# Second batch, chunks 0, 2 and 4: scores times v in three bfloat16 pieces instead of float32

## The chip, the cores and the metric

One Trainium2 chip, and one of its cores. The metric is the device time of one execution in microseconds (us): the median of several runs. The engines are PE (matrix products), PEld (PE's weight loads), DVE (vector), ACT (scalar), POOL (GpSimd) and SP, which issues all transfers (DMA) here. Each engine works through its own queue in order and waits on semaphores for the others.

## The reference

An attention with gates, 4 batches of 8 heads, 768 steps and 40 channels, and behind it a mixer of tokens and channels, all in float32:

```python
for t in range(S):
    m_new = np.maximum(f_gate[:, :, t] + m, i_gate[:, :, t])
    C = f_stab * C + i_stab * np.einsum('bhd,bhe->bhde', vt, kt)
    n = f_stab * n + i_stab * kt
    h_tilde = np.einsum('bhde,bhe->bhd', C, qt)
    denom = np.maximum(np.abs(nq), 1.0)          # nq: n times qt
    y[:, :, t] = o * h_tilde / denom             # o: sigmoid of o_gate
h = np.maximum(xt @ w_tok1, 0.0) @ w_tok2        # xt: y with steps last
u = x + h.transpose(0, 2, 1)
h2 = np.maximum(u @ w_ch1, 0.0) @ w_ch2
return (u + h2)
```

## The kernel before

A unit `(b, c)` is a batch `b` and a chunk `c` of 128 steps; there are 4 times 6. For a unit, PE makes the scores of 8 heads (`st_s`, tile `ps_sc`, L268). DVE multiplies them by decay weights (`st_p`, L278, two halves of four heads, in place in tile `dd`), which ACT has made as exponentials (`prep_exp`, L248, by halves) from what POOL has masked (`prep_mask`, L240). PE then multiplies the result by v with a column of ones (`st_pv`): 8 float32 products of 41 columns (L376), each two records in the trace. The share of the earlier chunks comes from a state `C` (product with q at L328 or L362; the update `pu` is L336 on PE, L340 and L344 on DVE). DVE divides (`st_norm`, L393 to L397, tile `x`), POOL multiplies by the gate (L404), ACT and POOL split x in two parts (`xh` L413, `xl` L418).

In the third and fourth batch (`three(u)`) the product with v is made in another way. The decayed scores are cut into three bfloat16 pieces: the upper 16 bits of the number as it stands, the upper 16 bits of the rest `r` (`prep_p2`, L290, two halves), and the rest of that (`prep_p3`, L298, two halves). v is cut into three as well (`prep_v`, L306 to L309, all on DVE). PE makes four bfloat16 products for a head (`st_pv3`, L357) into two PSUM tiles, ACT copies one column group (L364) and DVE adds the other (L365).

The mixer's products are L577, in dense streams: `gemm1` (tile `ps_h`, 16 products of 256 columns, read by ACT at L644 and by DVE at L645, tile `gl`) and `gemm2` (tile `acc`, two halves of 6 products of 320 columns; when a sum over 6 is ready, DVE adds it at L660 and so frees its PSUM bank). The order around the change is written out by hand. The attention of a batch is a generator, `att(b)`, with five pieces for a chunk: (0) scores, multiplication, `prep_p2`; (1) `prep_p3`, state; (2) exponentials of the next chunk's first half, its q and its weighted k; (3) product with v, `st_norm`; (4) `prep_v` of the next chunk, exponentials of its second half, loads. Batch 1 runs through its 30 pieces during the last six of the 18 steps of batch 0's mixer (`STEPS0`: how many pieces stand behind `gemm1`, behind the first and behind the second half of `gemm2`). Chunk 0's piece 0 stands one step earlier. PSUM pool `ps_m` has two banks, for `pu`, `po` and, in that one step, for two sums of `gemm2`.

Of the kernel before, what the change touches and what calls it, by code (L numbers as in the profile page):

```python
# [19 lines left out]
NC = S // L  # L20
# [14 lines left out]
def kernel(ctx: ExitStack, tc: tile.TileContext, gates, qk, q3, kv, og,  # L35
# [16 lines left out]
    def load_sig(b, i):  # L52
        t = ap.tile([128, NC // 2, DM], F32, tag="sig", name="sig", bufs=3)
        nc.sync.dma_start(out=t, in_=og[b].rearrange("(c p) e -> p c e", p=128)[:, 3 * i:3 * i + 3, :])
        sig[(b, i)] = t
# [93 lines left out]
    def top(x, i=1):  # L149
        return x.bitcast(BF16).rearrange("... (t i) -> ... t i", i=2)[..., i]  # L150
# [29 lines left out]
    def sigmoid(b, r=range(2), part=slice(0, 3)):  # L180
        for i in r:
            t = sig[(b, i)][:, part]
            nc.scalar.activation(t, t, AF.Sigmoid)
# [3 lines left out]
    def load_qk(u, hf):  # L187
        b, c = u
        t = T.setdefault(u, {})
        if hf == 0:  # L190
            t["raw"] = ap.tile([128, 2, 4, L], F32, tag="raw", name="raw", bufs=3)
        nc.sync.dma_start(out=t["raw"][64 * hf:64 * hf + D], in_=qk[b, c, hf])

    def load_phi(u):
        b, c = u
        T.setdefault(u, {})
        dd = ap.tile([128, H, L], F32, tag="dd", name="dd", bufs=3)
        if b:
            nc.sync.dma_start(out=dd, in_=phi_d[c, b * HP:b * HP + H].partition_broadcast(128))
        T[u]["dd"] = dd  # L200
# [7 lines left out]
    def load_q3(u):  # L208
        b, c = u
        if c > 0:  # L210
            load_pq(u, load_q3t(u))
# [16 lines left out]
    def prep_q3(u):  # L228
        if u[1] == 0:
            return  # L230
        q3t, pq = T[u]["q3"]
        nc.scalar.activation(pq, T[u].get("psq", pq), AF.Exp)  # L232
        if u[1] < NC - 1:
            T[u]["decay"] = a = ap.tile([120, 3], F32, tag="decay", name="decay")
            nc.gpsimd.tensor_copy(a, pq[:, :, L - 1])  # L235
        nc.gpsimd.tensor_tensor(q3t, q3t, pq, ALU.mult)  # L236

    def prep_mask(u):
        dd = T[u]["dd"]
        nc.gpsimd.affine_select(dd, dd, pattern=[[0, H], [1, L]], compare_op=ALU.is_ge,  # L240
                                fill=-1e30, base=0, channel_multiplier=-1)

    def prep_exp(u, hf):
        b, c = u
        dd = T[u]["dd"]
        src = T[u].get("phi")
        for h in range(4 * hf, 4 * hf + 4):
            nc.scalar.activation(dd[:, h, :], src[hf][:, h % 4, :] if src else dd[:, h, :], AF.Exp,  # L248
                                 bias=bcol[:, c, HP * b + h:HP * b + h + 1])

    def prep_kw(u):
        b, c = u
        if c == NC - 1:
            return
        t = T[u]
        kw = ap.tile([128, H * E1], F32, tag="kw", name="kw", bufs=2)
        kw = kw[:, 0:DM].rearrange("p (h d) -> p h d", d=D)
        nc.gpsimd.tensor_tensor(kw, t["kv"][:, 0:DM].rearrange("p (h d) -> p h d", d=D),
                                wcol[:, c, HP * b:HP * b + H].unsqueeze(2).to_broadcast([128, H, D]), ALU.mult)
        t["kw"] = kw  # L260

    def st_s(u, mult=True, mid=iter(())):
        t = T[u]
        t["s"] = [ps_s.tile([128, 4, L], F32, tag="s", name="ps_sc") for _ in range(2)]
        for h in range(4):
            for hf in range(2):
                r = t["raw"][64 * hf:64 * hf + D]
                nc.tensor.matmul(t["s"][hf][:, h, :], r[:, 1, h, :], r[:, 0, h, :], start=True, stop=True)  # L268
        if mult:
            st_p(u, mid)  # L270
# [7 lines left out]
            nc.vector.tensor_tensor(dd, t["s"][hf], dd, ALU.mult)  # L278

    def three(u):  # L280
        return u[0] > 1

    def prep_p2(u):
        t = T[u]
        dd = t["dd"]
        r = xpool[1].tile([128, H, L], F32, tag="p12", name="r", bufs=1)
        t["p"] = (top(dd), top(r), top(dd, 0))
        for hf in range(2):
            h = slice(4 * hf, 4 * hf + 4)
            nc.vector.tensor_tensor(r[:, h], dd[:, h], top(dd)[:, h], ALU.subtract)  # L290
        t["r"] = r

    def prep_p3(u):
        t = T[u]
        r, p3 = t["r"], t["p"][2]
        for hf in range(2):
            h = slice(4 * hf, 4 * hf + 4)
            nc.vector.tensor_tensor(p3[:, h], r[:, h], top(r)[:, h], ALU.subtract)  # L298

    def prep_v(u):  # L300
        t = T[u]
        vx = t["kv"][:, DM:]
        w = xpool[1].tile([128, 3, H * E1], BF16, tag="v3", name="v3", bufs=1)
        r = ap.tile([128, H * E1], F32, tag="kw", name="vr", bufs=2)
        v = nc.vector
        v.tensor_copy(w[:, 0], vx)  # L306
        v.tensor_tensor(r, vx, w[:, 0], ALU.subtract)
        v.tensor_copy(w[:, 1], r)
        v.tensor_tensor(w[:, 2], r, w[:, 1], ALU.subtract)  # L309
        t["v"] = w  # L310
# [8 lines left out]
    def st_state(u):  # L319
        b, c = u  # L320
        t = T[u]
        vx = t["kv"][:, DM:]
        t["C"] = Cst.get(b)
        if c > 0 and not three(u):
            po = po_tile(u)
            pof = po.rearrange("p h e -> p (h e)")
            for g, (h0, n) in enumerate(GR):
                nc.tensor.matmul(pof[:, h0 * E1:(h0 + n) * E1], t["q3"][0][0:n * D, g, :],  # L328
                                 Cst[b][0:n * D, g * G3:g * G3 + n * E1], start=g == 0, stop=False)
            t["po"] = po  # L330
        if c < NC - 1:
            pu = ps_m.tile([120, 3, G3], F32, tag="m", name="pu")
            puf = pu.rearrange("p g e -> p (g e)")
            kwf = t["kw"].rearrange("p h d -> p (h d)")
            for g, (h0, n) in enumerate(GR):
                nc.tensor.matmul(pu[0:n * D, g, 0:n * E1], kwf[:, h0 * D:(h0 + n) * D],  # L336
                                 vx[:, h0 * E1:(h0 + n) * E1], start=True, stop=True)
            cn = ap.tile([120, 3 * G3], F32, tag="C", name="Cn")
            for (p, a, z) in ((120, 0, 2 * G3), (80, 2 * G3, 2 * G3 + 2 * E1)):
                nc.vector.tensor_tensor(cn[0:p, a:z], puf[0:p, a:z], bm_t[0:p, a:z], ALU.mult)  # L340
            if c > 0:
                for g, (h0, n) in enumerate(GR):
                    sl = (slice(0, n * D), slice(g * G3, g * G3 + n * E1))
                    nc.vector.scalar_tensor_tensor(cn[sl], Cst[b][sl], t["decay"][0:n * D, g:g + 1], cn[sl],  # L344
                                                   op0=ALU.mult, op1=ALU.add)
            Cst[b] = cn
# [74 lines left out]
    def st_x(u):  # L421
        st_xm(u)
        st_xh(u)
        st_xl(u)

    units = [(b, c) for b in range(B) for c in range(NC)]
    u0, u1 = units[0], units[1]

    def after(u, n):
        i = units.index(u) + n  # L430
        return units[i] if i < len(units) else None

    def att(b):
        for c in range(NC):
            u = (b, c)
            n1, n2 = after(u, 1), after(u, 2)
            th = three(u)
            if b + 1 < B and c in (3, 4):
                load_sig(b + 1, c - 3)
            if b > 1 and c == 0:  # L440
                sigmoid(b)
            st_s(u)
            if n2:
                load_phi(n2)
            if n1 and not three(u):
                prep_mask(n1)
            if n2:
                load_qk(n2, 0)
            if th:
                prep_p2(u)  # L450
            yield
            if th:
                prep_p3(u)
            st_state(u)
            if n1 and three(u):
                prep_mask(n1)
            yield
            if n1:
                prep_exp(n1, 0)
                prep_q3(n1)  # L460
                prep_kw(n1)
            if n2:
                load_qk(n2, 1)
            yield
            st_pv(u)
            st_norm(u)
            if not th:
                st_x(u)
            yield
            if n1 and three(n1):  # L470
                prep_v(n1)
            if th:
                st_x(u)
            if n1:
                prep_exp(n1, 1)
            if n2:
                load_kv(n2)
                load_q3(n2)
            yield
# [296 lines left out]
    for c in range(2, NC - 1):  # L776
        u, n1, n2 = (units[c + i] for i in range(3))
# [225 lines left out]
```

## Time and profile before

| | |
|---|---|
| median of 3 runs | 459.84 us (455.59 to 465.8) |
| the profiled execution, its span | 459.81 us, 458.0 us |
| busy share of the span | PE 96%, PEld 92%, DVE 66%, ACT 43%, POOL 28% |
| granted PE clock, 40 equal slices, tenths | 9867779999999999999999999999999999999999 |
| chain that ended last, by engine | PE 74%, DVE 12%, DMA 6%, ACT 3%, POOL 3% |

And the stage in which the second batch's attention runs, by stretches (busy us of each engine, granted clock):

| us | PE | DVE | ACT | POOL | clock |
|---|---|---|---|---|---|
| 122 to 130 | 7.97 of 8 | 5.08 | 2.86 | 0.00 | 1.00 |
| 130 to 139 | 8.90 of 9 | 5.22 | 3.90 | 4.62 | 1.00 |
| 139 to 148 | 9.00 of 9 | 4.18 | 4.10 | 4.58 | 1.00 |
| 148 to 156 | 7.74 of 8 | 4.56 | 3.92 | 4.57 | 1.00 |
| 156 to 165 | 9.00 of 9 | 4.52 | 3.92 | 4.60 | 1.00 |
| 165 to 173 | 6.98 of 8 | 3.25 | 3.92 | 4.44 | 1.00 |

The span is the time from the first to the last instruction. Matrix products are pipelined and their ends are modelled, so PE's pace is read from the starts of its rows. In the clock's row a 9 is 90% or more of full speed.

### The profile page before, as it was taken

How to read it: one execution, taken by the hardware profiler on the slowest of the kernel's cores; microseconds unless marked ns; L12 is line 12 of the kernel's file. 1: busy time of each engine (PE TensorE's matmuls, PEld its weight loads, DVE VectorE, ACT ScalarE, POOL GpSimd, SP SyncE). 2: the span in 40 equal slices, each digit the busy share in tenths (PEclk: the TensorE clock that was granted, in tenths of full speed). 3: DMA queues.
4: the chain of work that ended last, by engine and by line, in shares of the span. 5: the costliest groups of instructions: out<-in, count | busy, mean ns of one | idle time of the engine just before them, and what ended most of it. 6: DMA issues, size and time to landing. Idle time of an engine off the chain costs nothing.

```text
span 458.0 us, 9425 instructions
## 1 busy us (share of the span) xinstructions
PE 441.7 (96%) x3713; PEld 421.6 (92%) x3713; DVE 303.7 (66%) x652; ACT 197.9 (43%) x478; POOL 130.2 (28%) x158
## 2 busy tenths in 40 slices
PE   8997897998999999999999999999999999999997
PEld 3887796998999989999999999999999999999996
DVE  5868789787455446879788667978888735233212
ACT  3665657997535355443242425532434212112111
POOL 5406423545334652142214402332412210000000
PEclk9867779999999999999999999999999999999999
DMA  7845757865066864323344422413421000000000
GB/s 181 249 130 159 221 163 243 285 177 159 0 208 191 248 220 124 106 105 94 107 148 135 154 87 75 136 33 92 161 73 38 1 2 29 1 1 29 1 31 29
DMA packets 24910, 52.98 MB, mean 116 GB/s; under 512 B 2574, under 2 KB 13658, under 8 KB 24866
## 3 DMA queue, kind: packets, MB, share of 16 engines
q1 hardware_dynamic: 24818, 52.27, 37.2%
q8 instruction: 29, 0.48, 0.4%
q14 instruction: 15, 0.12, 0.1%
q10 hardware_dynamic: 48, 0.11, 0.1%
HBM read 48.33 MB, written 4.04 MB: 114 GB/s over the span
## 4 chain that ended last, share of the span: by engine, by line
PE 74%; DVE 12%; DMA 6%; ACT 3%; POOL 3%; issue 2%; SPq 1%; DVEq 0%; ACTq 0%; POOLq 0%
PE ps_h L577 24%; PE acc L577 23%; PE ps_a L577 5%; PE ps_sc L268 4%; PE ps_b L577 4%; PE po L376 4%; DMA pq<-phi_d 3%; DVE wf L550 3%; PE po L357 3%; PE pu L336 2%; PE po L362 2%; DVE wf L554 2%; DMA wst<-in_wc_dram 2%; DVE r L290 1%; POOL q3t L236 1%
## 5 line engine op out<-in xcount | busy, mean ns | idle before, releaser
L577 PE MATMUL ps_h<-uT,c1h 128*128 128x256 f32 x720 | 140.2, 282 | 1.6 <-DVE uT L628 1.6
L577 PEld LDWEIGHTS ps_h<-uT,c1h 128*128 128x128 f32 x720 | 115.4, 188 | 2.4 <-DVE uT L628 1.8
L577 PE MATMUL ps_h<-uT,c1l 128*128 128x256 f32 x432 | 111.4, 280 | 0.0
L644 ACT ACTIVATE gh<-ps_h 128x512 fp32r<-128x512 f32 x72 | 42.5, 591 | 138.9 <-PE ps_h L577 138.9
L645 DVE SCALAR_TENSOR_TENSOR gl<-ps_h,gh 128x512 fp32r<-128x512 f32 x72 | 49.6, 688 | 77.7 <-ACT gh L644 77.5
L577 PE MATMUL acc<-c2h,gh 128*128 128x320 f32 x288 | 90.5, 322 | 0.0
L577 PE MATMUL acc<-c2l,gh 128*128 128x320 f32 x288 | 86.7, 309 | 0.0
L577 PEld LDWEIGHTS ps_h<-uT,c1l 128*128 128x128 f32 x432 | 81.4, 188 | 0.0
L577 PE MATMUL acc<-c2h,gl 128*128 128x320 f32 x288 | 66.1, 310 | 1.4 <-DVE gl L645 1.4
L577 PEld LDWEIGHTS acc<-c2h,gh 128*128 128x128 f32 x288 | 54.1, 188 | 1.3
L577 PEld LDWEIGHTS acc<-c2l,gh 128*128 128x128 f32 x288 | 54.2, 188 | 0.0
L577 PEld LDWEIGHTS acc<-c2h,gl 128*128 128x128 f32 x288 | 47.9, 188 | 2.5 <-DVE gl L645 2.3
L248 ACT ACTIVATE dd<-dd,bcol 128x128 f32<-128x128 f32 x144 | 45.7, 389 | 1.5 <-POOL dd L240 1.5
L278 DVE TENSOR_TENSOR dd<-ps_sc,dd 128x512 f32<-128x512 f32 x48 | 31.2, 683 | 21.5 <-ACT dd L248 13.0
L404 POOL TENSOR_TENSOR x<-x,sig 128x320 f32<-128x320 f32 x23 | 20.8, 904 | 56.7 <-DVE x L397 56.7
L235 POOL COPY decay<-pq 120x3 f32<-120x3 f32 x16 | 3.3, 208 | 113.4 <-ACT pq L232 89.9
L413 ACT ACTIVATE xh<-x 128x320 fp32r<-128x320 f32 x24 | 11.3, 470 | 52.3 <-POOL x L404 50.4
L268 PE MATMUL ps_sc<-raw 40*128 40x128 f32 x384 | 31.2, 298 | 2.6 <-DMA raw<-in_qk_dram 2.5
L268 PEld LDWEIGHTS ps_sc<-raw 40*128 40x128 f32 x384 | 25.9, 198 | 6.8 <-issue 2.5
L376 PE MATMUL po<-kvt,dd 128*128 128x41 f32 x192 | 29.4, 307 | 1.3 <-DVE dd L278 1.3
L376 PEld LDWEIGHTS po<-kvt,dd 128*128 128x128 f32 x192 | 28.2, 222 | 2.5 <-DVE dd L278 1.5
L236 POOL TENSOR_TENSOR q3t<-q3t,pq 120x384 f32<-120x384 f32 x20 | 22.0, 1098 | 26.5 <-ACT pq L232 22.4
(123 smaller groups left out, 777.5 us busy)
## 6 DMA issues: line engine op xcount, KB each, us to landing
dd<-phi_d SPq DMA_DIRECT2D x18, 512.0 KB
wst<-in_wc_dram SPq DMA_DIRECT2D x22, 384.0 KB
kvt<-in_kv_dram SPq DMA_DIRECT2D x24, 324.0 KB
raw<-in_qk_dram SPq DMA_DIRECT2D x48, 160.0 KB
sig<-in_og_dram SPq DMA_DIRECT2D x8, 480.0 KB
out_dram<-x SPq DMA_DIRECT2D x24, 160.0 KB
q3t<-in_q_dram SPq DMA_DIRECT2D x20, 180.0 KB
wst<-in_wt_dram SPq DMA_DIRECT2D x8, 384.0 KB
```

What stands on the lines that cost most here:

```text
L236: nc.gpsimd.tensor_tensor(q3t, q3t, pq, ALU.mult)
L248: nc.scalar.activation(dd[:, h, :], src[hf][:, h % 4, :] if src else dd[:, h, :], AF.Exp, bias=bcol[:, c, HP * b + h:HP * b + h + 1])
L268: nc.tensor.matmul(t["s"][hf][:, h, :], r[:, 1, h, :], r[:, 0, h, :], start=True, stop=True)
L278: nc.vector.tensor_tensor(dd, t["s"][hf], dd, ALU.mult)
L357: nc.tensor.matmul(po[:, h - h0, 0:j1 - j0], p[i][:, ROW[h], :], w[:, h, j0:j1], start=h == h0 and i + j0 == 0, stop=c == 0 and h == h1 - ...
L376: nc.tensor.matmul(po[:, h, :], t["dd"][:, ROW[h], :], vx[:, h * E1:(h + 1) * E1], start=c == 0 and h == 0, stop=h == H - 1)
L404: eng.tensor_tensor(x, x, sig[(b, c // 3)][:, c % 3, :], ALU.mult)
L413: nc.scalar.activation(xh, x, AF.Copy)
L550: v.scalar_tensor_tensor(fi, fi, 3, raw[:, :, 0], op0=ALU.logical_shift_left, op1=ALU.bitwise_or)
L577: nc.tensor.matmul(ps, a, m, start=(first and i == 0), stop=(last and i == n - 1))
L644: nc.scalar.activation(gh, ps, AF.Relu)
L645: nc.vector.scalar_tensor_tensor(gl, ps, 0.0, f32(gh), op0=ALU.max, op1=ALU.subtract)
```

## The change

Units (1, 0), (1, 2) and (1, 4) go the way of the last two batches: scores and v in three bfloat16 pieces. Unit (1, 0) has no chunk before it in which `prep_v` could stand, so its `prep_v` stands behind its `prep_p2`. All follows from `three`, by which `att`, `st_state` and `st_pv` choose.

```diff
     def three(u):
-        return u[0] > 1
+        return u[0] > 1 or u[0] == 1 and u[1] % 2 == 0
@@ att(b), piece 0
             if th:
                 prep_p2(u)
+            if th and u == units[NC]:
+                prep_v(u)
             yield
             if th:
                 prep_p3(u)
```

The two added lines move the numbers of the lines below them by two (L645 becomes L647, L660 becomes L662). ACT's, POOL's and SP's orders stay as they were, but for six L364 on ACT.

DVE's queue around chunk 0 of the second batch; `acc` are two finished sums of the mixer, `gl` the remainder that the mixer's next product needs, `Cn` the state. Before:

```order
L278 TENSOR_TENSOR dd<-ps_sc,dd 128x512 x2
L645 SCALAR_TENSOR_TENSOR gl<-ps_h_1596,gh 128x512
L660 TENSOR_TENSOR x<-acc_1107,x 128x320
L660 TENSOR_TENSOR x<-acc_1108,x 128x320
L340 TENSOR_TENSOR Cn<-pu,bm_t 120x246
```

And with the change:

```order
L278 TENSOR_TENSOR dd<-ps_sc,dd 128x512 x2
L290 TENSOR_TENSOR r<-dd 128x512 x2
L306 CAST v_1596<-kvt 128x328
L307 TENSOR_TENSOR vr<-kvt,v_1596 128x328
L308 CAST v_1596<-vr 128x328
L309 TENSOR_TENSOR v_1596<-vr,v_1596 128x328
L647 SCALAR_TENSOR_TENSOR gl<-ps_h_1602,gh 128x512
L662 TENSOR_TENSOR x<-acc_1107,x 128x320
L662 TENSOR_TENSOR x<-acc_1108,x 128x320
L298 TENSOR_TENSOR dd<-r 128x512 x2
L340 TENSOR_TENSOR Cn<-pu,bm_t 120x246
```

Six operations now stand between the multiplication and the two additions that free PSUM banks, and two more between these and the state.

DVE's queue from chunk 1's division to chunk 2's state. Before:

```order
L397 TENSOR_TENSOR x<-po,den 128x320
L278 TENSOR_TENSOR dd<-ps_sc,dd 128x512 x2
L645 SCALAR_TENSOR_TENSOR gl<-ps_h_1808,gh 128x512
L340 TENSOR_TENSOR Cn<-pu,bm_t 120x246
L340 TENSOR_TENSOR Cn<-pu,bm_t 80x82
```

And with the change:

```order
L397 TENSOR_TENSOR x<-po,den 128x320
L306 CAST v_1814<-kvt 128x328
L307 TENSOR_TENSOR vr<-kvt,v_1814 128x328
L308 CAST v_1814<-vr 128x328
L309 TENSOR_TENSOR v_1814<-vr,v_1814 128x328
L278 TENSOR_TENSOR dd<-ps_sc,dd 128x512 x2
L290 TENSOR_TENSOR r<-dd 128x512 x2
L647 SCALAR_TENSOR_TENSOR gl<-ps_h_1855,gh 128x512
L298 TENSOR_TENSOR dd<-r 128x512 x2
L340 TENSOR_TENSOR Cn<-pu,bm_t 120x246
```

The split of v stands in front of the multiplication, L290 right behind it, and `gl` of the mixer between L290 and L298. Chunks 3 and 4 read the same.

## Rows read from the trace of the kernel before

**Rows 1.** Chain that ended last: start us, us, what.

```profile
137.33 1.73 PE po L376 x16
...
192.40 1.02 PE po L357 x32
```

**Rows 2.** PE's timeline: start, length (us), line, operation, out<-in, count [idle before].

```profile
132.81 1.16 PE L268 MATMUL ps_sc<-raw 40*128 40x128 f32 x16
...
138.87 0.39 PE L577 MATMUL acc<-c2h,gh 128*128 128x320 f32 x1
...
147.86 0.39 PE L577 MATMUL acc<-c2h,gh 128*128 128x320 f32 x1
...
155.43 0.39 PE L577 MATMUL acc<-c2h,gh 128*128 128x320 f32 x1
...
164.32 0.39 PE L577 MATMUL acc<-c2h,gh 128*128 128x320 f32 x1
...
170.68 1.53 PE L376 MATMUL po<-kvt,dd 128*128 128x41 f32 x12 [1.02 <-DVE dd L278]
...
172.04 0.39 PE L577 MATMUL acc<-c2h,gh 128*128 128x320 f32 x1
```

**Rows 3.** DVE's timeline, chunks 0 and 1 of the second batch.

```profile
126.22 1.29 DVE L278 TENSOR_TENSOR dd<-ps_sc,dd 128x512 f32<-128x512 f32 x2 [0.16 <-PE ps_sc L268]
...
129.74 1.01 DVE L660 TENSOR_TENSOR x<-acc,x 128x320 f32<-128x320 f32 x2
...
133.62 0.49 DVE L397 TENSOR_TENSOR x<-po,den 128x320 f32<-128x320 f32 x1
...
136.76 0.69 DVE L278 TENSOR_TENSOR dd<-ps_sc,dd 128x512 f32<-128x512 f32 x1 [1.97 <-ACT dd L248]
...
139.85 0.49 DVE L397 TENSOR_TENSOR x<-po,den 128x320 f32<-128x320 f32 x1
```

**Rows 4.** The split of v: DVE's timeline, and the view of line L307.

```profile
173.29 0.32 DVE L306 CAST v<-kvt 128x328 bf16<-128x328 f32 x1
...
175.10 1.06 DVE L309 TENSOR_TENSOR v<-vr,v 128x328 bf16<-128x328 f32 x1
...
L307 DVE TENSOR_TENSOR vr<-kvt,v x12: 501/984/1267, 173.7 to 360.6; 128x328 f32<-128x328 f32 x12
```

**Rows 5.** POOL's and DVE's timeline in the third batch.

```profile
203.62 1.02 POOL L236 TENSOR_TENSOR q3t<-q3t,pq 120x384 f32<-120x384 f32 x1
...
203.67 2.65 DVE L290 TENSOR_TENSOR r<-dd 128x512 f32<-128x512 f32 x2
...
206.24 1.36 DVE L298 TENSOR_TENSOR dd<-r 128x512 bf16<-128x512 f32 x2
...
217.44 1.28 DVE L290 TENSOR_TENSOR r<-dd 128x512 f32<-128x512 f32 x2
```

**Rows 6.** PE and DVE around the product in three pieces, third batch.

```profile
207.65 0.24 PE L357 MATMUL po<-v,dd 128*128 128x41 bf16 x2 [0.20 <-DVE dd L298]
...
209.07 0.39 PE L577 MATMUL acc<-c2h,gh 128*128 128x320 f32 x1
...
194.85 0.49 DVE L397 TENSOR_TENSOR x<-ht,den 128x320 f32<-128x320 f32 x1
```

**Rows 7.** PE's timeline where the clock fell or held; two stretches, PEclk third from last.

```profile
56.44 0.90 PE L328 MATMUL po<-Cn,q3t 120*128 120x123 f32 x6 [1.23 <-POOL q3t L236]
...
60.93 0.47 PE L577 MATMUL ps_a<-xh,w1l 128*128 128x320 f32 x1
...
64.40 0.37 PE L577 MATMUL ps_a<-xl,w1h 128*128 128x320 f32 x1
...
76.60 0.71 PE L577 MATMUL ps_h<-uT,c1h 128*128 128x256 f32 x3 [1.58 <-DVE uT L628]
...
58.00:59.00 1.00, 1.00 (x8) 1.00 (x7) 1.00 (x3) 1.00 (x4) 0.47 (x1) 0.50 0.85 299
...
76.00:77.00 1.00, 0.40 (x3) 0.38 (x3) 0.94 (x4) 1.00 (x3) 1.00 (x2) 1.00 0.85 286
```

## Prediction, made before the changed kernel was run

> **What bounds the kernel now.** I read the table of the profile first: PE is busy for 96% of the span, and in the stage that the change touches, 124 to 173 us, it is busy 98 to 100% of each stretch, but for the last chunk. There PE works in a fixed order on two things: the second matrix product of the first batch's tail, and the six attention chunks of the second batch. So I read next the times at which PE leaves each chunk's product of scores and v [rows 2]. Each row is the first instruction of PE behind the 16 records of L376, so the ends are, for chunks 0 to 5: 132.81, 138.87, 147.86, 155.43, 164.32 and 172.04. The last steps are 8.99, 7.57, 8.89 and 7.72 us long, and in the last PE waits 1.02 us for DVE in front of L376 (the row at 170.68). That row matters more than its size: it shows that the scores arrive only just in time. The DVE rows [rows 3] say the same of chunk 1: its second multiplication L278 begins at 136.76, and PE is through with the whole product 2.1 us later. So PE is full, but the chain from scores to product has almost no slack. Work put on that chain, between L278 and the product, is paid in PE time.
>
> **What the change removes.** For chunks 0, 2 and 4 the 16 float32 records (1.73 us) become 32 bfloat16 ones (1.02 us) [rows 1]. That is 0.71 us less PE work for a chunk, 2.1 us for three. The inter-chunk product with the state (L328, now L362) moves behind the scores' product and keeps its records. PE gains this only where it doesn't wait.
>
> **What it adds.** On DVE, for each such chunk: the L290 pair at 1.28 us, the L298 pair at 1.36 [rows 5], four operations that split v, which take from 173.29 to 176.16, so 2.87 us with their gaps [rows 4], and two L365. On ACT two L364. That is 6 us of DVE a chunk against some 4.5 us of DVE work in 9 us now, so DVE as a whole still fits. What counts is where they stand in DVE's queue (the order rows above).
>
> **Chunk 0.** The L278 pair ends at 127.51 (126.22 + 1.29) [rows 3]. Behind it now stand L290 (1.28), the split of v, the gl of the next product (0.69) and the L660 pair (1.01), and only then L298 (1.36). PE is late twice: its state product pu takes the PSUM bank that L660 frees, and the bfloat16 product needs L298. The split of v has two bounds: 2.87 as in the row, or 1.76 if L307 and L309 take the shortest time seen, 0.50 each instead of 1.05 and 1.06 [rows 4]. POOL stands idle from 122 to 130 us (the table), so I take a value near the lower. L298 then ends at 133.6 to 134.7. Behind it come, in the row of a later chunk, 1.47 us until PE is through (207.60 to 209.07) [rows 6], here about 0.9, as chunk 0 has no state product. Chunk 0 ends at 134.9 (134.5 to 135.6) instead of 132.81: **+2.1**.
>
> **Chunk 1** keeps float32, but its chain hangs on chunk 0: ACT computes the second half of its exponentials only behind xh of chunk 0. From the end of the bfloat16 product to x it takes 1.92 us (193.42 to 195.34, the rows of the third batch) [rows 1, 6], from x to the second L278 2.65 (134.11 to 136.76) [rows 3], then 0.69 for it and 1.36 for the last 12 records (170.68 to 172.04) [rows 2]: 6.7 us against a step of 6.06 before. Chunk 1 ends at 141.6: +2.7.
>
> **Chunks 2 and 4.** The chain from the light chunk before: 1.47 to x (138.87 to 140.34) [rows 2, 3], 2.87 for the split of v, which stands in front of the next L278 pair, then L278 1.29, L290 1.28, gl 0.69, L298 1.36, and 1.47 for PE behind it [rows 3 to 6]: 10.43 us. The steps before were 8.99 and 8.89, so these chunks add 1.4 and 1.5. ACT's exponentials are ready by then: x to L278 takes 2.65, less than the split of v with the first L278 behind it. **Chunk 3** hangs on chunk 2 by the 6.7 us above, under its old step of 7.57, so it keeps the old step. **Chunk 5** loses the stall of 1.02, as 6.7 us fit PE's own 6.70. Sum of the steps: 2.1 + 0.6 + 1.4 + 0 + 1.5 - 1.0 = **+4.6**.
>
> **Port.** An L290 pair took 2.65 us at 203.67, where POOL ran q3t from 203.62 on, and 1.28 at 217.44 [rows 5]. So DVE's operations with two SBUF inputs lose up to 1.37 us to POOL for a pair. In the stage POOL is busy half of the time, with just such work. In chunks 2 and 4 I take half the loss, 0.7 each, between the bounds 0 and 1.37: **+1.4**. The Trainium skill, "SBUF — State Buffer", section "Who interferes with whom", says that a VectorE instruction with two SBUF inputs and a GpSimd instruction that reads SBUF block each other in full, the second waiting for the first. It speaks against this change, which adds twelve L290 and L298 and six L307 and L309 to such a stage; the trace agrees (2.65 against 1.28). With a whole pair blocked in both chunks the sum would be 1.3 us more.
>
> **Clock.** In the stage the granted clock is 1.00 throughout, and the change puts waits of 2 us or more of PE into three places. After an idle time of 1.23 us (at 56.44) among attention products the clock fell to 0.50, that is to 1.2 GHz; after one of 1.58 us at 76.60, among dense products, it stayed at 1.00 [rows 7]. At 0.50 the dense products from 60.93 to 64.40 went in 13 steps of 0.267 us, half speed: 3.5 us of such work lost 1.7 us. I take that as the price of one fall, and one fall as likeliest: **+1.7**, bounds 0 and 5.1.
>
> **The sum.** 4.6 + 1.4 + 1.7 = 7.7 us on top of the profiled execution's 459.81 us (a span of 458.0, and 1.8 around it), which differs from the median of the runs shown, 459.84, by 0.03. Behind chunk 5 I see no wait of PE that could take the delay back. **Predicted: 467.5 us**, slower by 1.7%.
>
> **Rivals.**
> - *The chain, and no fall of the clock*: 4.6 + 1.4 = 6.0, so 465.8. For it: the 1.58 us without a fall, and dense products on both sides of each wait. Chance 0.27.
> - *The likeliest, one fall or two*: 467.5 to 469.2. Chance 0.38.
> - *Everything late*: the port costs the whole 1.37 twice and the clock falls at all three waits: 4.6 + 2.7 + 5.1 = 12.4, so 472.2. For it: the waits then reach 3 us, longer than any that kept the clock. Chance 0.25.
> - *PE hides it* (the other side): PE's own work in the steps of chunks 2 and 4 is 8.2 us (8.89 - 0.71). If the DVE chain of 10.43 fell under that, all DVE work would lie under dense products and only the saving would be left: 459.8 - 2.1 = 457.7, no change that can be told. It decides at 2.2 us less in the chain, as by a split of v that takes 1.76 and ran before the old multiplications needed DVE. DVE idles for 2 us in front of the second L278 (to 136.76), which speaks for it; that the split alone fills this gap, and L290 and L298 come behind it, speaks against it. Chance 0.10, a part of it for gains that I don't see.
>
> **Range and chances.** Low end: the chain alone, without port or clock and with the shorter split, 464.2, and below it a part of the hidden case: 462.5. High end 474.5, past the case in which all is late. A measurement of this kernel tells about 2% from no change, which is 9.2 us, so 469.0 us. Slower by over 2%: nearly the whole third rival and 0.35 of the likeliest, 0.38 in all. Faster by over 2%: 0.04, since the whole saving is 2.1 us. Within 2%: 0.58.
>
> **What would show it.** Right, if in the new profile: the L357 records of the second batch wait for L298 by 1.5 to 3.5 us in chunks 2 and 4; pu of chunk 0 starts at about 132 instead of 130.32 behind a late L660; DVE is busy without a gap from the second L278 of a light chunk to the L365 of the heavy one; chunk ends stand at about 134.9, 141.6, 152.7, 160.3, 171.4 and 178.1 before any fall of the clock; and everything behind 173 us is only shifted. Wrong, if L357 starts without waits for DVE (then PE hid the work), if the split of v takes 1.8 us in chunks 2 and 4 too (2.2 us less in all), or if the granted clock leaves 1.00 for more than 7 us at a time.

## The result, and the profile after

| | before | changed |
|---|---|---|
| median, 16 executions each | 457.31 us (455.55 to 465.80) | 465.09 us (459.49 to 474.35) |
| profiled execution, its span | 459.81, 458.0 | 460.91, 459.1 |
| busy share | PE 96%, DVE 66% | PE 95%, DVE 70% |

The ratio is 1.0122, with a 95% interval of 1.0087 to 1.0157: the change costs time, less than the 2% that count as a difference here. (The ratio leaves out executions over 1.5% above the fastest of their kernel; the medians and the table of all runs below hold every one.) Predicted were 467.5 us, with a range of 462.5 to 474.5.

The profiled execution is only 1.1 us longer than that of before, and is one of the fastest of the changed kernel. Its page has the granted clock by 40 slices:

```profile
PEclk9996689999999999999999999999999999999999
```

In the trace of before the clock was low three times in the start-up and at the last instant; here only twice. Each execution is listed with its span and its mean granted clock. With the two levels of 1.2 and 2.4 GHz, the time at the low one is 2 x (1 - clock) x span: 28.4 us in the profiled execution of before (clock 0.969), 20.2 in this one (0.978). So the two profiles can't be compared by their totals, only by stages. PE's rows in the second batch, with the chunk ends as in [rows 2] (the first row behind each product of scores and v) and the waits of PE of over half a us:

```profile
128.57 0.80 PE L336 MATMUL pu<-kvt,kw 128*120 128x123 f32 x6 [1.27 <-POOL decay L235]
...
130.75 0.24 PE L357 MATMUL po<-v,dd 128*128 128x41 bf16 x2 [0.72 <-DVE dd L298]
...
131.55 1.16 PE L268 MATMUL ps_sc<-raw 40*128 40x128 f32 x16
...
137.05 1.53 PE L376 MATMUL po<-kvt,dd 128*128 128x41 f32 x12 [0.61 <-DVE dd L278]
138.41 0.40 PE L579 MATMUL acc<-c2h,gh 128*128 128x320 f32 x1
...
146.87 0.24 PE L357 MATMUL po<-v,dd 128*128 128x41 bf16 x2 [1.61 <-DVE dd L298]
...
148.92 0.39 PE L579 MATMUL acc<-c2h,gh 128*128 128x320 f32 x1
...
156.04 0.39 PE L579 MATMUL acc<-c2h,gh 128*128 128x320 f32 x1
...
164.24 0.24 PE L357 MATMUL po<-v,dd 128*128 128x41 bf16 x2 [1.46 <-DVE dd L298]
...
166.27 0.39 PE L579 MATMUL acc<-c2h,gh 128*128 128x320 f32 x1
...
173.18 0.40 PE L579 MATMUL acc<-c2h,gh 128*128 128x320 f32 x1
```

The scores of chunk 0 begin at 121.81 here and at 124.73 before. From there to the end of chunk 5 it takes 51.37 us; before it took 47.31. **The stage grew by 4.06 us.** The six steps are 9.74, 6.86, 10.51, 7.12, 10.23 and 6.91, against 8.08, 6.06, 8.99, 7.57, 8.89 and 7.72. The 1.27 at 128.57 is put down to POOL, but `decay` had been written by 128.01: the bank of `pu` came free when L662 had read it, late behind L290 and the split of v. In the traces of before, changed, e1, e4, e6 and e7 alike, `pu` starts 0.58 or 0.59 us behind the start of this pair (L660 in the kernel before). DVE in chunk 0, first a row of the kernel before, where it had 1.62 us to spare, then the changed kernel:

```profile
129.13 0.69 DVE L645 SCALAR_TENSOR_TENSOR gl<-ps_h,gh 128x512 fp32r<-128x512 f32 x1 [1.62 <-ACT gh L644]
```

```profile
124.51 1.28 DVE L290 TENSOR_TENSOR r<-dd 128x512 f32<-128x512 f32 x2
125.71 0.32 DVE L306 CAST v<-kvt 128x328 bf16<-128x328 f32 x1
...
127.39 0.68 DVE L647 SCALAR_TENSOR_TENSOR gl<-ps_h,gh 128x512 fp32r<-128x512 f32 x1
127.99 0.88 DVE L662 TENSOR_TENSOR x<-acc,x 128x320 f32<-128x320 f32 x2
128.79 1.91 DVE L298 TENSOR_TENSOR dd<-r 128x512 bf16<-128x512 f32 x2
```

DVE in chunk 2 (compare the last two rows of [rows 3], and [rows 4] for the split):

```profile
139.39 0.49 DVE L397 TENSOR_TENSOR x<-po,den 128x320 f32<-128x320 f32 x1
139.80 0.44 DVE L306 CAST v<-kvt 128x328 bf16<-128x328 f32 x1
140.35 0.83 DVE L307 TENSOR_TENSOR vr<-kvt,v 128x328 f32<-128x328 f32 x1
141.22 0.88 DVE L308 CAST v<-vr 128x328 bf16<-128x328 f32 x1
142.13 0.50 DVE L309 TENSOR_TENSOR v<-vr,v 128x328 bf16<-128x328 f32 x1
142.55 0.68 DVE L278 TENSOR_TENSOR dd<-ps_sc,dd 128x512 f32<-128x512 f32 x1
143.62 0.69 DVE L278 TENSOR_TENSOR dd<-ps_sc,dd 128x512 f32<-128x512 f32 x1 [0.39 <-ACT dd L248]
144.23 1.34 DVE L290 TENSOR_TENSOR r<-dd 128x512 f32<-128x512 f32 x2
145.50 0.68 DVE L647 SCALAR_TENSOR_TENSOR gl<-ps_h,gh 128x512 fp32r<-128x512 f32 x1
146.10 1.35 DVE L298 TENSOR_TENSOR dd<-r 128x512 bf16<-128x512 f32 x2
```

From the end of x (139.88) to the end of L298 (147.45) DVE does nothing else and waits once, 0.39 us, for ACT. The L290 pair takes 1.34 and the L298 pair 1.35, as in the third batch without POOL beside them (1.28 and 1.36 in [rows 5]).

**All executions, at an equal clock.** A straight line through the executions of all kernels of this study, with one slope and a constant for each kernel, says that an us at the low clock costs 0.36 us of time (what is left over scatters by 0.8 us). So each kernel has two numbers: its time at an equal clock, against before, and its mean time at the low clock. The errors are those of the mean. The kernel before ran again beside each group of experiments, 87 times in all; at an equal clock it differs by at most 0.3 us between the groups. The 16 executions of before in the first table are not among the 87, as their clock is not on record; their mean is 457.98 us.

| kernel | executions | median us | at an equal clock, us | mean time at the low clock, us |
|---|---|---|---|---|
| before | 87 | 457.75 | 0 | 25.3 ± 0.9 |
| changed | 16 | 465.09 | +4.5 ± 0.2 | 32.9 ± 2.9 |
| e1, chunk 0 alone | 12 | 462.14 | +2.3 ± 0.2 | 28.8 ± 2.3 |
| e2, chunks 2 and 4 alone | 12 | 462.48 | +3.1 ± 0.3 | 28.1 ± 1.8 |
| e3, split of v early | 6 | 465.51 | +5.1 ± 0.5 | 33.9 ± 5.1 |
| e4, PE's part alone | 12 | 461.01 | +0.2 ± 0.2 | 32.9 ± 2.7 |
| e5, waits filled | 12 | 461.04 | +4.1 ± 0.2 | 22.3 ± 2.2 |
| e6, no L290, L298 | 13 | 459.73 | +0.3 ± 0.3 | 31.9 ± 2.8 |
| e7, no split of v | 12 | 462.02 | +2.4 ± 0.3 | 28.9 ± 1.9 |
| e8, e3 and exponentials early | 6 | 464.44 | +4.9 ± 0.3 | 28.4 ± 2.9 |
| e9, before, exponentials early | 12 | 455.47 | -1.6 ± 0.1 | 22.8 ± 2.2 |
| e10, changed, exponentials early | 6 | 468.01 | +3.7 ± 0.2 | 39.4 ± 4.6 |
| e11, e2 and exponentials early | 6 | 464.06 | +3.2 ± 0.4 | 34.4 ± 4.8 |
| e12, e10 and a later product | 6 | 467.09 | +3.7 ± 0.2 | 35.2 ± 2.9 |

The changed kernel's mean is 466.07 us, 7.25 over the 458.82 of before: 4.5 at an equal clock, which is the 4.06 of the stage and little else, and 0.36 x 7.6 = 2.7 from 7.6 us more at the low clock (7.6 ± 3.0, so 2.7 ± 1.1). The profiled executions agree: 459.81 + 4.06 - 0.36 x 8.2 = 460.9.

### The profile page after: what moved, and what is told of

It reads as the page before. It is cut to its first block, busy times and chain, and to the rows that moved or that the text cites. A ratio compares the mean times of both kernels' runs of the same rounds, so it can differ in the third digit from the quotient of the medians.

```text
span 459.1 us, 9557 instructions
## 1 busy us (share of the span) xinstructions
PE 437.4 (95%) x3761; PEld 417.2 (91%) x3761; DVE 321.5 (70%) x682; ACT 199.8 (44%) x484; POOL 132.3 (29%) x158
## 4 chain that ended last, share of the span: by engine, by line
PE 66%; DVE 17%; DMA 6%; issue 4%; ACT 3%; POOL 3%; SPq 0%; DVEq 0%; POOLq 0%; ACTq 0%
PE ps_h L579 23%; PE acc L579 22%; PE ps_a L579 5%; DMA pq<-phi_d 4%; PE ps_b L579 3%; PE ps_sc L268 3%; DVE wf L552 3%; PE po L357 3%; DVE r L290 2%; PE po L362 2%; PE po L376 2%; DMA wst<-in_wc_dram 2%; DVE dd L278 1%; DVE dd L298 1%; DVE wf L556 1%
## 5 line engine op out<-in xcount | busy, mean ns | idle before, releaser
L647 DVE SCALAR_TENSOR_TENSOR gl<-ps_h,gh 128x512 fp32r<-128x512 f32 x72 | 49.6, 689 | 76.0 <-ACT gh L646 75.9
L278 DVE TENSOR_TENSOR dd<-ps_sc,dd 128x512 f32<-128x512 f32 x48 | 31.2, 682 | 10.9 <-ACT dd L248 6.5
L552 DVE SCALAR_TENSOR_TENSOR wf<-wf,wst 128x384 int32<-128x384 int32 x30 | 22.8, 780 | 6.4 <-POOL c2l L573 2.1
L357 PE MATMUL po<-v,dd 128*128 128x82 bf16 x360 | 21.2, 188 | 4.7 <-DVE dd L298 4.6
```

The costliest lines, as they stand in the source:

```text
L357: nc.tensor.matmul(po[:, h - h0, 0:j1 - j0], p[i][:, ROW[h], :], w[:, h, j0:j1], start=h == h0 and i + j0 == 0, stop=c == 0 and h == h1 - ...
L552: v.scalar_tensor_tensor(fi, fi, 3, raw[:, :, 0], op0=ALU.logical_shift_left, op1=ALU.bitwise_or)
L647: nc.vector.scalar_tensor_tensor(gl, ps, 0.0, f32(gh), op0=ALU.max, op1=ALU.subtract)
```

## Experiments

The theories: **chain** (PE stands still for DVE's work between scores and product; in the form A the split of v carries the cost, in the form B the pieces of the scores behind the second L278 do), **clock** (the waits also let the granted clock fall in part of the executions), and against both that PE hides the work, or that the cost lies in the products themselves.

### e1 and e2: one half of the change each

```diff
-        return u[0] > 1 or u[0] == 1 and u[1] % 2 == 0
+        return u[0] > 1 or u == (1, 0)                # e1
+        return u[0] > 1 or u in ((1, 2), (1, 4))      # e2
```

> Only chunk 0 of the second batch is done in three pieces, with its own split of v; chunks 2 and 4 stay float32. Chain theory (PE stands still for DVE's work between scores and product, and that is all): in the changed kernel PE waits 1.27 us in front of pu and 0.72 in front of L357 in this chunk and saves 0.3 of work, and chunk 1 follows 0.8 late, so about +2 us on the kernel before with the granted clock as it was, and no wait for L298 before the third batch but this one. Clock theory (the waits also let the granted clock fall in part of the executions): on top of this a mean clock that differs by 0.01 and more from execution to execution, with 1 to 10 us. If PE hid the work: no more than the kernel before.

> Only chunks 2 and 4 of the second batch are done in three pieces; chunk 0 stays float32. Chain theory: PE waits 1.6 to 1.8 us for L298 in each of the two chunks, saves 0.3 of work in each and loses the stall of 1.0 us in chunk 5: 3.5 - 0.6 - 0.8, so about +2 us on the kernel before at a steady clock. With e1 the two parts add up to the 4.1 us by which the stage grew in the changed kernel. Clock theory: these are two waits among attention products, so it is here that the mean granted clock of the executions spreads (0.94 to 0.98), with up to 10 us more; in e1, with one wait, less.

Measured: ratios 1.0069 [1.0024, 1.0114] and 1.0097 [1.0059, 1.0135]; at an equal clock +2.3 and +3.1. Both halves cost, each about as the chain theory has it, e2 a us more. The sum is 5.4, 0.9 more than the whole. A part of that is in e2's chunk 2, where PE waits 0.47 us for L290 and then 1.61 + 0.20 for L298, against 1.61 + 0.21 above. Both traces also caught a fall of the clock in the stage, right behind the waits. The stretches of e2 around its chunk 2, with busy time of PE, PEld, DVE, ACT and POOL and then the granted clock:

```profile
138.00:143.00 5.00, 3.59 (x31) 3.30 (x30) 4.56 (x8) 3.40 (x10) 2.65 (x3) 1.00 0.82 199
143.00:145.00 2.00, 1.13 (x23) 1.01 (x24) 2.00 (x5) 0.52 (x1) 1.12 (x2) 1.00 0.52 195
145.00:149.00 4.00, 4.00 (x32) 3.63 (x32) 2.90 (x9) 0.61 (x2) 1.71 (x3) 0.57 0.32 79
```

PE is busy 3.59 us of 5 and 1.13 of 2, waiting for DVE; from 145 the clock is low, and dense products that start every 0.148 us in the trace after stand 0.27 apart. In e1 it was low for 6.8 us from 131.7 on, when the second of the two waits of chunk 0 was ending.

### e4, e6 and e7: leave out DVE's work, all of it or one half

```diff
 def prep_p2(u):                               # e4 and e6
+    if u[0] == 1:
+        t["p"] = (top(dd),) * 3
+        return
 def prep_p3(u):                               # e4 and e6
+    if u[0] == 1:
+        return
 def prep_v(u):                                # e4 and e7
+    if u[0] == 1:
+        t["v"] = top(vx).unsqueeze(1).to_broadcast([128, 3, H * E1])
+        return
```

> PE's part of the change alone: chunks 0, 2 and 4 run the 32 bfloat16 products of L357 and the state product behind them, with ACT's and DVE's merge L364 and L365, but DVE computes no second and third pieces of scores and v (no L290, L298, split of v): PE reads the first piece each time. Chain theory: with DVE's work gone nothing waits, and the time is that of the kernel before less PE's saving, 0.8 us by the busy time of the two traces, 2.1 by the prediction's rows: 455 to 457 with the clock as in the kernel before. Clock theory: the same, with no spread of the granted clock. If the small products themselves cost the time, or let the clock fall: several us over the kernel before, as in the changed kernel.

> The changed kernel without L290 and L298 in the second batch: the scores' second and third pieces aren't computed and PE reads the first piece each time; the split of v is there, in its place. Theory A (the split of v in front of L278 carries the cost, as the prediction's chain of 10.43 us has it): 2.8 us a chunk stay on the chain, so +2 to +3 on the kernel before at an equal clock. Theory B (the split lies beside the way from x over POOL and xh to ACT's second half of the exponentials, which ends about as late; L290 and L298 behind the second L278 carry it): +0 to +1, as with no DVE work at all (e4).

> The changed kernel without the split of v in the second batch: v's second and third pieces aren't computed and PE reads the first piece each time; L290 and L298 are there. Theory A: 2.8 us leave the chain of chunks 2 and 4 and 1.66 that of chunk 0; about the time of the kernel before, +0 to +1 at an equal clock. Theory B: L278 waits for ACT's exponentials instead, as in e3; only chunk 0 gains its 1.3 to 1.7 us, so +3 at an equal clock, and L357 of chunks 2 and 4 still waits 1.3 to 1.8 us for L298.

Measured at an equal clock: +0.2 without any of it, +0.3 with the split of v alone, +2.4 with the pieces of the scores alone, +4.5 with both. So the cost is DVE's work, not the products. But the two halves don't add up: the split alone costs nothing, and on top of L290 and L298 it costs 2.1. Most of the 2.1 is chunk 0's: there DVE had 1.62 us to spare in front of `gl`, so the split alone (1.76, e6) or L290 alone (1.28, e7) left the two additions and with them `pu` where they were; PE waited for nothing there in e6, and 0.17 us in e7. Both together don't fit, and it waits 1.27 and 0.72. In chunks 2 and 4 theory A falls (it wanted +2 to +3 for e6 and no more than +1 for e7), and B is right for chunk 2. DVE there in e6:

```profile
143.14 0.49 DVE L402 TENSOR_TENSOR x<-po,den 128x320 f32<-128x320 f32 x1
143.55 0.32 DVE L311 CAST v<-kvt 128x328 bf16<-128x328 f32 x1
...
146.12 1.06 DVE L314 TENSOR_TENSOR v<-vr,v 128x328 bf16<-128x328 f32 x1
147.10 0.68 DVE L278 TENSOR_TENSOR dd<-ps_sc,dd 128x512 f32<-128x512 f32 x1
148.53 0.69 DVE L278 TENSOR_TENSOR dd<-ps_sc,dd 128x512 f32<-128x512 f32 x1 [0.75 <-ACT dd L248]
```

The split takes 3.6 us here, as POOL works beside it, and still the second L278 waits another 0.75 us for ACT's exponentials. They hang on the same x by another way: POOL's product with the gate (in POOL's queue behind q3t and kw), ACT's xh, then the second half. In the changed kernel that way ends at 143.62, and but for it L278 could have begun at 143.2, behind the split and the first half. The split lies **beside** it. In e7's chunk 2 PE accordingly still waits 1.60 us for L298; in chunk 4 it waits 0.56, but there the clock had been low from 155 to 162, so that PE came late itself. What e7 gains for sure is chunk 0: the 1.27 in front of pu is gone, and of 0.72 in front of L357 0.17 are left.

e4 shows a second thing: PE's saving doesn't come out. The rows of its stage in which PE waits, in chunks 1, 2, 3 and 5:

```profile
135.24 1.53 PE L384 MATMUL po<-kvt,dd 128*128 128x41 f32 x12 [0.55 <-DVE dd L278]
...
143.89 0.71 PE L365 MATMUL po<-kvt,dd 128*128 128x82 bf16 x16 [0.39 <-DVE dd L278]
...
152.77 1.53 PE L384 MATMUL po<-kvt,dd 128*128 128x41 f32 x12 [1.36 <-DVE dd L278]
...
171.01 1.53 PE L384 MATMUL po<-kvt,dd 128*128 128x41 f32 x12 [0.16 <-DVE dd L278]
```

PE is through earlier with the heavy chunks and waits for the second L278 instead: 2.46 us in four places against 1.28 in two before. The chain by x, POOL and ACT is what PE runs into as soon as it is faster.

### e3, e8, e10, e12: move the work

```diff
 # e3, e8: split v of chunks 2 and 4 between the two L278 of the chunk before
-            st_s(u)
+            early = n1 and b == 1 and c < NC - 1 and three(n1)
+            st_s(u, mid=(prep_v(x) for x in (n1,) if early))
-            if n1 and three(n1):
+            if n1 and three(n1) and not early:
                 prep_v(n1)
 # e8, e9, e10, e11, e12: ACT's second half two pieces ahead, in front of xh
                 prep_kw(n1)
+                if b == 1 and n1[0] == 1:
+                    prep_exp(n1, 1)
-            if n1:
+            if n1 and not (b == 1 and n1[0] == 1):
                 prep_exp(n1, 1)
 # e12: half a dense product ahead of the product of chunks 2 and 4
-    STEPS0 = ((0, 0, 6), (2, 1, 1), (0, 3, 2), (3, 2, 0), (0, 3, 2), (3, 1, 0))
+    STEPS0 = ((0, 0, 6), (2, 1, 1), (0, 1, 4), (3, 2, 0), (0, 1, 4), (3, 1, 0))
```

> The changed kernel, but DVE splits v of chunks 2 and 4 one chunk earlier, between the two L278 of the light chunk, where it waits 2.20 and 1.73 us for ACT's exponentials; chunk 0 is as in the changed kernel. Chain theory: 2.83 us leave the chain from the light chunk's x to L298, so L357 of chunks 2 and 4 waits for 0 to 0.3 us instead of 1.6 to 1.8, while the light chunk's second L278 comes 0 to 0.6 late: 2 to 3 us less than the changed kernel at a steady clock, +1 to +2 on the kernel before. Clock theory: with two of the three waits gone, the mean granted clock spreads less and the median comes nearer to the kernel before by more than those 3 us. If the cost is DVE's total or the port and not the place in the queue: no gain.

> The changed kernel with the split of v early (e3) and with ACT's second half of the exponentials of chunks 1 to 5 moved two pieces ahead, behind kw and in front of xh of the chunk before, so that it no longer waits for x and POOL. Theory B: the second L278 follows the first at once, L290 and L298 run 1 to 2 us earlier, L357's waits in chunks 2 and 4 fall under 0.5 us and those of L376 in the light chunks vanish: at an equal clock 2 to 4 us less than the changed kernel, so +0 to +2 on the kernel before, perhaps under it. If L278 then waits for the scores (PE itself) or ACT's new order delays gh of the dense product: less gain, with new waits of PE for gh or gl.

> The changed kernel with that new order of ACT alone; the split of v stays behind x of the light chunk, where in e8's trace DVE waited 3.3 us for the scores. Theory B: the split fits into that wait, both L278 of chunks 2 and 4 follow the scores at once, and L357 there waits 0.3 to 1.0 us instead of 1.6 to 1.8; the light chunks' waits (0.61 and 0.19) go too: 2 to 3 us less than the changed kernel at an equal clock, +1.5 to +2.5 on the kernel before, nearly all of it chunk 0's. Theory A (the split in DVE's queue carries it): no gain.

> e10 with one more change: in PE's order the second half of the dense product (0.9 us) stands in front of the product of scores and v of chunks 2 and 4, not behind it. In e10 and in the changed kernel PE has only 2.9 us of dense work and 0.6 of state product between the end of the scores and L357, and DVE puts L278, L290, gl and L298 into that. Distance theory (what counts is the work of PE between scores and product against DVE's chain, and the split of v and ACT's exponentials end about together, so that moving either alone gains nothing): L357's waits in chunks 2 and 4 fall by 0.9 us each, the light chunks have slack for it, and the time is 1.5 to 2 us less than e10 at an equal clock, about +2 on the kernel before. If DVE's whole work of a pair of chunks sets the step: the 0.9 us comes back as a wait of the next light chunk in front of L376, and the time is that of e10, +3.8.

None of the four gained what was hoped for: +5.1, +4.9, +3.7 and +3.7 at an equal clock, against +4.5. In each the wait moved, and the trace says where to. In **e3** chunk 4 has its split behind it, and DVE waits for ACT in its place:

```profile
162.58 0.69 DVE L278 TENSOR_TENSOR dd<-ps_sc,dd 128x512 f32<-128x512 f32 x1 [2.06 <-ACT dd L248]
```

And PE, in chunks 1 and 4:

```profile
136.82 1.53 PE L376 MATMUL po<-kvt,dd 128*128 128x41 f32 x12 [1.76 <-DVE dd L278]
...
165.82 0.24 PE L357 MATMUL po<-v,dd 128*128 128x41 bf16 x2 [1.61 <-DVE dd L298]
```

L357 still waits 1.61 us. In chunk 2 it waits 0.57, where PE came late itself, as the clock was low for 3.4 us from 138.7 on. And the early split pushed the second L278 of the light chunks back: PE lost 1.76 us in chunk 1 and 0.85 in chunk 3. "No gain" is what this run's rival, DVE's total, had said; but DVE is not full here, it stands idle for the 2.06 us. **e8** takes away both ways. L357 waits only 0.57 and 0.64 in front of chunks 2 and 4 (the first of them after a fall of the clock again, the second at full clock), and chunk 4 takes 9.41 us. But now the light chunks' exponentials are early too, and the split, in front of their second L278, is the only thing that holds it: PE waits 1.96 and 0.83 there. **e10** puts the split back behind x. ACT is waited for no more; DVE's chunk 2:

```profile
140.54 0.32 DVE L306 CAST v<-kvt 128x328 bf16<-128x328 f32 x1
...
142.90 1.05 DVE L309 TENSOR_TENSOR v<-vr,v 128x328 bf16<-128x328 f32 x1
143.88 1.27 DVE L278 TENSOR_TENSOR dd<-ps_sc,dd 128x512 f32<-128x512 f32 x2
145.08 2.17 DVE L290 TENSOR_TENSOR r<-dd 128x512 f32<-128x512 f32 x2
...
147.77 1.34 DVE L298 TENSOR_TENSOR dd<-r 128x512 bf16<-128x512 f32 x2
```

And POOL beside it:

```profile
141.69 0.99 POOL L258 TENSOR_TENSOR kw<-kvt,wcol 128x320 f32<-128x320 f32 x1
142.64 0.96 POOL L404 TENSOR_TENSOR x<-x,sig 128x320 f32<-128x320 f32 x1
...
145.01 1.09 POOL L240 TENSOR_SCALAR_AFFINE_SELECT dd<-dd 128x1024 f32<-128x1024 f32 x1
```

The split takes 3.4 us beside POOL's kw and x, and the L290 pair 2.17 beside the mask. From the end of x to that of L298 it is 8.5 us, against 7.57 in the changed kernel, where the wait for ACT had kept L290 back until 144.23, when the mask (143.33 to 144.43) was nearly done. The light chunk's earlier end bought little: L357 of chunk 2 waits 0.93 for L290 and 1.60 for L298. In **e12** the half of a dense product took the place of the 0.93, and chunk 3's scores began 0.94 us earlier, counted from the end of chunk 1 (11.61 against 12.55). In chunk 4 the split (3.4, against 2.74 in e10) and L290 (2.17 against 1.81) then took it back: L357 waits 1.57. The distance theory falls in this form. Its rival had the time right (+3.8), but not the wait: no light chunk waits longer than 0.21. In e10 and e12 how long PE waits is set by DVE's row of work from x to L298, whose length depends on what POOL does beside it.

### e11: chunks 2 and 4 with the exponentials early

The diff is that of e2 with that of e10.

> The same new order of ACT with chunks 2 and 4 in three pieces and chunk 0 in float32 (e2 with ACT's new order). Theory B: what is left of e10 without chunk 0's waits: 0 to -1 us on the kernel before at an equal clock, 3 to 4 us less than e2. Theory A: as e2, +3.

Measured: 464.06 us, ratio 1.0103 [1.0036, 1.0170], +3.2 at an equal clock. As e2, which is what form A had said: with ACT out of the way the split of v is on the path after all. But the split is not alone in it. From the end of x to that of L298 DVE takes 7.96 us in chunk 2 and 8.46 in chunk 4, against 8.07 and 7.07 in e2: beside POOL's mask the L298 pair of chunk 2 took 2.29 and the L290 pair of chunk 4 2.17. So in chunks 2 and 4 A and B are two branches of one chain that end together, and taking ACT's away also brings DVE's operations against POOL's. How much of the missing gain is the one and how much the other, no run takes apart.

### e5: fill PE's waits

```diff
+    def fill(u, n):
+        z = id_t.bitcast(BF16)
+        t = T[u]["s"][1].rearrange("p h t -> p (h t)")[:, 0:256]
+        for i in range(n):
+            nc.tensor.matmul(t, z[:, 0:128], z, start=i == 0, stop=i == n - 1)
+            if u == units[NC]:            # in front of st_state
+                fill(u, 10)
+            if th and b == 1:             # in front of st_pv
+                fill(u, 12 if c else 6)
```

> The changed kernel with dense bfloat16 products that nothing reads, put into PE's order where it waits: 10 of 256 columns in front of pu of chunk 0, 6 in front of its L357, 12 in front of those of chunks 2 and 4 (0.107 us each at full clock, so 1.1, 0.6 and 1.3 us, against waits of 1.27, 0.72 and 1.6 to 1.8). They need no result of the chain. Clock theory: PE no longer stands still, so the granted clock falls no more often than in the kernel before (a mean low time near its 26 us instead of the 33 of the changed kernel), and the median comes 2 to 3 us under the changed kernel, while the fitted time at an equal clock stays 4 to 5 us over the kernel before. If the falls have nothing to do with the waits: same spread as the changed kernel, and no gain.

Measured: 461.04 us, ratio 1.0072 [1.0037, 1.0108], against 1.0122 for the changed kernel. At an equal clock it is as slow as the changed kernel within 0.4 us (+4.1); the time at the low clock is 22.3 us instead of 32.9, no more than before. So 0.36 x 10.6 = 3.8 us came back by products that nothing reads, since the granted clock fell less. (The difference of 10.6 is three times its error of 3.6.) The stage of its trace, in two stretches, columns as above:

```profile
131.00:155.00 24.00, 22.23 (x238) 20.64 (x237) 20.26 (x46) 10.95 (x31) 11.43 (x15) 1.00 0.63 191
155.00:180.00 25.00, 24.33 (x237) 22.77 (x237) 18.96 (x47) 12.11 (x35) 12.69 (x15) 1.00 0.71 201
```

### e9: the kernel before, with the exponentials early

> The kernel before, with only ACT's order changed: the second half of the exponentials of the second batch's chunks 1 to 5 stands behind kw, in front of xh of the chunk before. Theory B (the way from x over POOL and xh to the exponentials is what the second L278 waits for): DVE's waits for ACT in front of L278 (13.0 us in five in the kernel before) go, and with them PE's two stalls in front of L376 (0.26 and 1.02): 1.0 to 1.3 us less than the kernel before at an equal clock. If ACT's new order delays gh or q3t: new waits of PE for gl or q3t, and no gain.

Measured: 455.47 us, ratio 0.9947 [0.9918, 0.9977], -1.6 us at an equal clock: the fastest kernel of the study. DVE's waits in its stage, from the view of waits (us in total, times, longest); in the kernel before, the view of the stage has L278 wait for ACT five times, 13.0 us in all:

```profile
DVE dd L278 <- PE ps_sc L268: 5.1, 5, 1.9
DVE dd L278 <- ACT dd L248: 0.3, 1, 0.3
```

PE's two stalls in front of L376 (0.26, and 1.02 in [rows 2]) are gone; from the scores of chunk 0 to the end of chunk 5 it is 45.56 us. There PE waits for nothing that the profile shows.

## Why the prediction held, step by step

**The sum.** Predicted +7.7 as 4.6 (steps) + 1.4 (port) + 1.7 (clock). Measured, over all executions, +7.25, as 4.5 at an equal clock and 2.7 by the clock. The likeliest rival was the right one: PE waits for the chain, and the clock falls in part of the executions. e4, e6 and e7 show the first part, e5 the second. That the sum fits so well is in part luck: the port's 1.4 was hardly there, and the clock took 1.0 more. The time itself came out 2.4 us under 467.5, since the profiled execution of 459.81, on which the sum was put, lies 2.5 above the median of 457.31. "PE hides it" is out (e1 and e2, each slower), and so is "everything late" as the usual case (waits of 3 us and three falls a run).

**Chunk 0: right, for the reason named.** Predicted +2.1; the step is 1.66 longer, and e1 has +2.3 in all. pu waited for the bank behind the late L662, L357 for L298, and the split took its short form (1.76 us, the lower bound), POOL being idle.

**Chunk 1:** predicted +0.6, measured +0.80 (the four terms add up to 6.62, not 6.7). **Chunks 2 and 4:** predicted 10.43 us of chain, measured 10.51 and 10.23 (+1.52 and +1.34, for +1.4 and +1.5), with waits for L298 of 1.82 and 1.66, inside the 1.5 to 3.5 that were named. **Chunk 3:** 0 predicted, -0.45 measured. **Chunk 5:** -1.0 predicted, -0.81 measured. The sum of the steps was 4.6, measured 4.06.

**The split of v: right in size, wrong in weight.** The prediction put it into the chain as 2.87 us (measured 2.83 in chunk 2) and took ACT's exponentials for ready by then, by 2.65 against 3.56. In the changed kernel they were not ready: the second L278 waited 0.39 us for them. The 2.65 was chunk 1's row. In that trace, of the kernel before, it is 5.41 in chunk 2 (140.34 to 145.75) and 4.63 in chunk 4, as ACT's `pq` waited 1.61 and 1.14 us there for a DMA, and POOL's product with the gate stands in its queue behind what needs `pq`. In chunk 2:

```profile
140.79 0.52 ACT L232 ACTIVATE pq<-pq 120x384 f32<-120x384 f32 x1 [1.61 <-DMA pq<-phi_d]
```

```profile
145.75 0.69 DVE L278 TENSOR_TENSOR dd<-ps_sc,dd 128x512 f32<-128x512 f32 x1 [2.96 <-ACT dd L248]
```

In the changed kernel ACT didn't wait for that DMA in front of chunks 2 and 4, and x to the second L278 took 3.74 and 3.62. With 5.41 the chain would have been some 1.8 longer (an estimate: 5.41 - 3.56), so that about 10.43 came out is in part luck. As it is, the two ways end within half a us, and e3 and e7 show that in chunk 2 or 4 taking the split out moves little. The rival in which PE hides the work was to decide "by a split of v that takes 1.76 and ran before the old multiplications needed DVE". That is e3, and there L357 of chunk 4 waits 1.61 us instead of 1.46.

**PE's saving: mis-sized.** 0.71 us a chunk was taken from [rows 1]. In e4's chunk 4, where PE doesn't wait, state update, products and L362 take 2.41 us (163.09 to 165.50) against 2.97 in the kernel before (161.35 to 164.32, with L328): 0.56. And e4 shows that of 1.7 us for three chunks nothing arrives.

**Port: mis-sized, +1.4 for what was about nothing on top of the chain.** L290 and L298 took 1.33 to 1.35 in chunks 2 and 4, one L298 pair 1.91 in chunk 0 beside POOL's kw. What DVE lost beside POOL in chunks 2 and 4 was in the split (2.83 in chunk 2, 1.76 in chunk 0), and the chain's 2.87 already held that. The Trainium skill, "SBUF — State Buffer", section "Who interferes with whom", was right as a rule: in e10 the same L290 pair takes 2.17 us beside POOL's mask. What the prediction lacked was the moment. The wait for ACT in front of L278 held L290 until POOL's mask was nearly done.

**Clock: +1.7 for 2.7, within the error of 1.1.** One fall was taken as the usual case, with 1.7 us. In the traces of e1, e2, e3, e4, e6, e7, e8 and e11 the clock is low in the stage, for 3.4 to 10.2 us at a time, or 13.6 in two falls (e3); in those of before, changed, e5, e9, e10 and e12 it is not. The prediction called it wrong if the clock left 1.00 for more than 7 us at a time; e3's second fall did that (10.2 us), the changed kernel's own trace shows no fall in the stage. No profile was taken of one of its executions with a fall in the stage; that its 7.6 us lie there rests on the eight traces and on e5.

**The chunk ends** were named on the time axis of before, with the port in them: 134.9, 141.6, 152.7, 160.3, 171.4 and 178.1. With 2.92 us added for the earlier start of the scores the measured ones are 134.5, 141.3, 151.8, 159.0, 169.2 and 176.1. The last two are 2 us early: the port's 1.4, and chunk 3's step, which was not kept but 0.45 shorter.

## What to carry to other kernels

Leaving out one piece at a time can mislead. Two pieces may each fit into an engine's idle time and together overrun it (chunk 0), and where an engine waits for a chain with two branches that end together, taking one away gains little (chunks 2 and 4): leave out pieces in all combinations (e4, e6, e7) before a cost is put on one. DVE was not full (busy 41.7 of the 51.4 us of the stage); PE paid because the work stands between a product and the product that reads it. That another place would have been free is not shown: none of the orders tried for the whole change came under +3.7. And look at what the chain hangs on before the change: moving one ACT operation ahead of another that waited for POOL (e9) gave 0.5%, where the new form of the product cost 1.2%.

## What the runs showed of the hardware

- The granted clock fell to half behind waits of PE shorter than the 1.58 us that had left it at full speed in [rows 7]: 0.83 us in e6, and 1.36 in e4, where it is 0.57 over 154 to 162. Columns as above, e4:

```profile
149.00:154.00 5.00, 3.64 (x34) 3.53 (x33) 2.96 (x7) 3.28 (x10) 2.77 (x3) 1.00 0.90 237
154.00:162.00 8.00, 8.00 (x46) 7.45 (x46) 2.89 (x9) 2.28 (x7) 4.58 (x6) 0.57 0.81 232
162.00:165.00 3.00, 3.00 (x45) 2.99 (x44) 1.83 (x6) 2.17 (x6) 0.28 (x1) 1.00 0.50 162
```

  Not each such wait is followed by a fall: e10 and e12 have waits of 1.5 to 1.6 us and none in the stage of their traces.

- The kernel before alone scatters between 14 and 45 us at the low clock, and the others scatter as widely; falls in the start-up, which the change doesn't touch, make much of that: in the profiled executions they take from 17 us (e2) to 41 (e7). It is a scatter of 11 us in the time, and to compare kernels at an equal clock brings it down to 0.8.
- An operation with one SBUF input was slower beside POOL as well: the cast L308 took 0.33 us in chunk 0, with no row of POOL beside it, and 0.88 in chunk 2 beside POOL's product with the gate (140.79 to 141.91). No run tests this by itself.
